# Joining softmax half rows with one-operand VectorE forms, and finishing the attention output on GpSimd

## The chip, the cores and the metric

The kernel runs on one core of a Trainium2 chip. The metric is device time in microseconds (us) from start to end of one execution. The engines named below are TensorE (PE in the profile, with its weight loads on a row of their own, PEld), VectorE (DVE), ScalarE (ACT), GpSimd (POOL) and the queue engine SyncE (SP), which here issues every DMA of the kernel. Each engine takes its instructions strictly in the order in which they stand; a semaphore wait of one instruction holds everything behind it on that engine.

## The reference, cut to what matters

Two independent results are put side by side. The left half is attention with 32 heads of 32 columns that share one key and one value head; the right half is a two-dimensional real Fourier mixing, written as matrix products.

```python
q = (x @ wq) split into 32 heads          # x: 2048 x 1024
k = x @ wk ; v = x @ wv                   # 2048 x 32 each
p = softmax(q k^T * 32**-0.5)             # per head, 2048 x 2048
a = concat_heads(p v) @ wo
y = Cr @ (xb @ Wr^T) - Ci @ (xb @ Wi^T)   # 2048 x 1024, Cr and Ci 2048 x 2048
out = concatenate([a, y], axis=-1)
```

## The kernel before, in words

All products outside the score and value products are made of three terms: an operand is cast to a rounded high part, the rest is its low part, and high·high, low·high and high·low are added in PSUM. In the profile's names `rh`, `rl` are the high and low part of a right operand, `mh`, `ml` of a left one.

The attention is cut into 32 units, one for each of four blocks of 512 queries (b) and eight groups of four heads (g). A unit passes through two loops of 32 steps each.

- The score loop, `score_step(s)`: a step makes the scores of 128 queries of one head against half of the 2048 keys (two matmuls into `pss`). VectorE takes the negative maximum of that half row into `nm` (a reduce of 128x1024 from PSUM). One step later ScalarE exponentiates the half row in place with that maximum as bias and leaves the sum of the half row in `ls`. So for each row there are two maxima and two sums.
- The join. When a unit's 32 score steps are through, its half rows are joined. The step number behind that is `e`: at e=1 `lse_1` finds the joint minimum of the negative maxima (`mm`) and the two differences (`md`); at e=2 `lse_1b` exponentiates the differences on ScalarE; at e=3 `lse_2` multiplies with the half sums, adds them (`l`), splits the joint maximum into a rounded and a low part and takes the reciprocal of the sum, all three into one tile `m`; at e=6 `lse_3` turns this tile with a TensorE transposition into a PSUM bank `psb` and VectorE copies it to `mt`; at e=8 `lse_4` sends two parts of `mt` by DMA into two rows of the query tile `qst` (so that the next product subtracts the maximum by itself) and the third part to memory.
- The value loop, `expo(n)` and `pv`: scores are made again, transposed (two matmuls into `pst`), exponentiated by ScalarE into `p`, and every eighth step the products with `v` go to `psb` and are added up in `ov` by VectorE. `expo` of unit u begins at e=12 of that unit, and its first matmul reads the two rows of `qst`. Score steps of the next unit and value steps of this one are recorded alternately, in one loop over n. After a unit's last `pv`, the next three steps take one entry each from the list `ends`: `ov` times 1/sum (`rb`, which the function `inverse` loads), the cast to the high part `oh`, and the low part `ol`. The low part's entry also records the stores of both parts on SP.

Between these steps the function `take` records the fill: about five matmuls per step of the other products (projections, the Fourier mixing, the output product), in groups of 24 or 12 matmuls to one PSUM bank. There are two such banks; the transposition and `pv` use them too. A group's result is taken out by VectorE. `aside()` runs before the transposition and before `pv`: close to a group's end it first takes the group's remaining matmuls, close to its begin the first six.

The fill's operands are prepared by two lines of due times (`RL`, `ML`, with leads counted in fill matmuls): SP loads a source into a staging tile, GpSimd adds or subtracts a second source where there is one (`r<-r,r`, `m<-m,m`), casts (`rh`, `mh`) and makes the low part (`rl`, `ml`). Left sources are loaded 52 matmuls ahead and prepared 36 to 21 ahead, right sources loaded and combined 40 ahead and finished 14 to 8 ahead. The staging tiles are few (`NR0, NM0 = 3, 3`), so a load on SP waits until GpSimd has made the low part of an earlier operand; all later DMAs stand behind that load. Stores stand nine fill matmuls behind the instruction that makes their data (`BEHIND = 9`). All engines but the DMA hardware keep program order.

Of the kernel before, what the change touches and what calls it, by code (L numbers as in the profile page):

```python
# [8 lines left out]
F32 = mybir.dt.float32  # L9
F32R = mybir.dt.float32r  # L10
AF = mybir.ActivationFunctionType
ALU = mybir.AluOpType
AX = mybir.AxisListType
# [3 lines left out]
P = 128  # L17
# [7 lines left out]
NC = 16  # L25
# [62 lines left out]
def tile_kernel(ctx: ExitStack, tc, xT, wq, wkv, wo, xbT, wT, cT, out):  # L88
    nc = tc.nc
    te = Ordered(tc, nc.tensor)  # L90
    act = Ordered(tc, nc.scalar)
    dve = Ordered(tc, nc.vector)
    gp = Ordered(tc, nc.gpsimd)
# [3 lines left out]
    def pool(stack, name, bufs, **kw):  # L97
        kw.setdefault("reuse_waits", "tile")
        return stack.enter_context(tc.tile_pool(name=name, bufs=bufs, **kw))
# [14 lines left out]
    ident = keep.tile([P, P], F32, name="ident")  # L114
# [17 lines left out]
    op = pool(ctx, "op", 2, side="right")  # L132
    hp = pool(ctx, "hp", 1, side="right")

    def move(q, to, of):
        q.dma_start(to.bitcast(F32), of.bitcast(F32))
# [181 lines left out]
    def store(to, of, key=None):  # L318
        def go():
            move(sp, to, of)  # L320
            if key:
                ready.add(key)
        soon(go)
# [4 lines left out]
    def bank(name, open_=False):  # L328

        b = 1 - cur["bank"] if cur["bank"] is not None else int(used[1] < used[0])  # L330
        cur["at"] += 1
        used[b] = cur["at"]
        if open_:
            cur["bank"] = b
        return ps_b[b].tile([P, W], F32, name=name)
# [42 lines left out]
    def aside():  # L378

        if cur["group"] >= len(groups):  # L380
            return
        g = groups[cur["group"]]
        j = pos["fill"] - g.at
        if 0 < j < 6:
            take(6 - j)
        elif j > g.n - 6:
            take(g.n - j)
# [193 lines left out]
    sm = pool(ctx, "sm", 2)  # L581
    onp = pool(ctx, "onp", 1)

    units = [(b, g) for b in range(NQ) for g in range(NG)]
# [3 lines left out]
    qst, nm, ls, lse, pt, ov, rb, pend = ({} for _ in range(8))  # L588
    ends = []

    def open_unit(u):
        b, g = units[u]
        assert ("q", b, g) in ready
        q = qsp.tile([P, 4, W], F32R, name="qst")
        gp.memset(q[96:P].bitcast(F32), 0.0)
        for r, src in enumerate((qh_d, ql_d, qh_d)):
            move(sp, q[r * DH:(r + 1) * DH], src[b][g].rearrange("(h d) c -> d h c", d=DH))
        qst[u] = q
        nm[u] = sm.tile([P, 2, NC], F32, name="nm")
        ls[u] = sm.tile([P, 2, NC], F32, name="ls")  # L600

    def scores(s):
        u, r = divmod(s, SU)
        i, j = divmod(r, 2)
        h, t = divmod(i, 4)
        ps = ps_s.tile([P, 2 * W], F32, name="pss")
        for a in range(2):
            k0 = (2 * j + a) * W
            te.matmul(ps[:, a * W:(a + 1) * W], qst[u][:, h, t * P:(t + 1) * P], kst[:, k0:k0 + W], start=True, stop=True)
        dve.tensor_reduce(nm[u][:, j, i:i + 1], ps, axis=AX.X, op=ALU.max, negate=True)  # L610
        pend[s] = ps

    def row_sums(s):
        if s not in pend:
            return
        ps = pend.pop(s)
        u, r = divmod(s, SU)
        i, j = divmod(r, 2)
        act.activation(ps, ps, AF.Exp, bias=nm[u][:, j, i:i + 1], accum_out=ls[u][:, j, i:i + 1])

    def lse_1(u):
        m = sm.tile([P, NC], F32, name="mm")
        d = sm.tile([P, 2, NC], F32, name="md")
        dve.tensor_tensor(m, nm[u][:, 0], nm[u][:, 1], op=ALU.min)
        for j in range(2):
            dve.tensor_sub(d[:, j], m, nm[u][:, j])
        lse[u] = m, d

    def lse_1b(u):
        act.activation(lse[u][1], lse[u][1], AF.Exp)  # L630

    def lse_2(u):
        m, d = lse[u]
        l = sm.tile([P, NC], F32, name="l")
        m2 = sm.tile([P, 3, NC], F32, name="m2")
        dve.tensor_mul(d, d, ls[u])
        dve.tensor_add(l, d[:, 0], d[:, 1])
        dve.tensor_copy(m2[:, 0].bitcast(F32R), m)
        dve.tensor_sub(m2[:, 1], m, m2[:, 0])
        dve.reciprocal(m2[:, 2], l)  # L640
        lse[u] = m2

    def lse_3(u):
        m2 = lse.pop(u)
        aside()
        pm = bank("psb")
        te.transpose(pm[:3 * NC, :P], m2.rearrange("p a b -> p (a b)"), ident)
        mt = sm.tile([3 * NC, P], F32, name="mt")
        dve.tensor_copy(mt, pm[:3 * NC, :P])
        cur["at"] += 1  # L650
        lse[u] = mt

    def lse_4(u):
        mt = lse.pop(u)
        for a in range(2):
            move(sp, qst[u][96 + a:97 + a].rearrange("o h (t c) -> o (h t) c", c=P), mt[a * NC:(a + 1) * NC])
        sp.dma_start(r_d[u], mt[2 * NC:])
# [16 lines left out]
    def pv(u, k):  # L674

        aside()
        ps = bank("psb")
        for c in range(4 * k, 4 * k + 4):
            for h in range(4):
                te.matmul(ps[h * DH:(h + 1) * DH], v[:, c], pt[u, c, h // 2][:, h % 2], start=c == 4 * k, stop=c == 4 * k + 3)  # L680
        if k == 0:
            ov[u] = onp.tile([P, W], F32, name="ov")
            dve.tensor_copy(ov[u], ps)
        else:
            dve.tensor_add(ov[u], ov[u], ps)
        cur["at"] += 1
        if k == NC // 4 - 1:
            b, g = units[u]
            hi_ = onp.tile([P, W], F32R, name="oh")
            lo_ = onp.tile([P, W], F32R, name="ol")  # L690
            lse["out"] = hi_, lo_

            def low():
                dve.tensor_sub(lo_, ov[u], hi_.bitcast(F32))
                if u + 1 < len(units):
                    store(oh_d[b][g], hi_)
                    store(ol_d[b][g], lo_, ("o", b, g))

            ends.append(lambda: dve.tensor_mul(ov[u], ov[u], rb[u]))
            ends.append(lambda: dve.tensor_copy(hi_, ov[u]))  # L700
            ends.append(low)

    def score_step(s):

        if s < total:
            u, r = divmod(s, SU)
            if r == SU - 6 and u + 1 < len(units):
                open_unit(u + 1)
            scores(s)
        row_sums(s - 1)  # L710
        u, e = divmod(s - SU, SU)
        if 0 <= u < len(units):
            if e == 1:
                lse_1(u)
            elif e == 2:
                lse_1b(u)
            elif e == 3:
                lse_2(u)
            elif e == 6:
                lse_3(u)  # L720
            elif e == 8:
                lse_4(u)


    room = [(lambda t=t, k=k: t[:, k]) for t in [pp.tile([P, 2, W], F32, name="p") for _ in range(9)] for k in range(2)]
    room += [(lambda t=t: t) for t in [hp.tile([P, W], F32, name=f"h{k}") for k in range(8)]]
# [5 lines left out]
    pump()  # L732
    take(START)
    open_unit(0)
    take(66)
    for s in range(SU + LEAD):
        score_step(s)
        take(7)
# [14 lines left out]
    for n in range(total):  # L753
        u, r = divmod(n, SU)
        if n == total - 12:
            w1 = wo_set(1)
            add([o_group(NQ - 1, t, e, ws) for e, ws in ((0, w0), (1, w1)) for t in range(4)])
        score_step(n + SU + LEAD)
        if ends:
            ends.pop(0)()  # L760
        expo(n)
        if r == 16:
            inverse(u)
        if r % 8 == 0 and n:
            pv(*divmod(n // 8 - 1, 4))
        level(n)


    last = groups[len(groups) - 8:]
    take(last[0].at - pos["fill"] - 12)  # L770
    pv(len(units) - 1, 3)
    while ends:
        ends.pop(0)()
# [65 lines left out]
```

## Time and profile before

| | us |
|---|---|
| three runs before | 2829.01, 2833.28, 2835.64; median 2833.28 |
| profiled execution, whole | 2835.39 |
| its span from first to last instruction | 2833.5 |
| PE busy in the span | 2780.5 (98%) |
| VectorE busy | 1733.6 (61%) |
| ScalarE busy | 2187.6 (77%) |
| GpSimd busy | 1481.7 (52%) |

The span is first to last instruction of the profiled execution, 1.9 us less than its own time. Every operation goes through one recording helper, so all have the line L66, and groups are told apart by tile names instead. A unit takes some 82 us. Units are counted from 0; unit 21 is the sixth head group of the third query block.

### The profile page before, as it was taken

The numbers are of one execution on the slowest core, as the hardware profiler recorded it, in microseconds if no ns is written. First come the engines' busy times: TensorE is split into PE (matmuls) and PEld (weight loads), VectorE is DVE, ScalarE is ACT, GpSimd is POOL, SyncE is SP. The second block draws the span as 40 slices with busy tenths as digits, with TensorE's granted clock in tenths as the row PEclk, the third lists the DMA queues.
The fourth block names the chain that finished last, engine by engine and source line by source line (L and its number), as shares of the span: only waits on it lengthen the run. The fifth ranks groups of instructions, "written<-read, shape, count | busy, mean of one in ns | idle before, by whom it ended". The sixth has DMA issues, their size and how long they took to land.

```text
span 2833.5 us, 40225 instructions
## 1 busy us (share of the span) xinstructions
PE 2780.5 (98%) x13904; PEld 1931.6 (68%) x13904; DVE 1733.6 (61%) x1925; ACT 2187.6 (77%) x3151; POOL 1481.7 (52%) x1433
## 2 busy tenths in 40 slices
PE   7999999999999999999999999999999999999999
PEld 5776666767666676767676766666666666767656
DVE  5766666666676666656665665666666566656511
ACT  4578888888888788888787877788878888888740
POOL 2321134565534447767685565787888765630010
PEclk9999999999999999999999999999999999999999
DMA  8865435775576455544463454564554543554445
GB/s 294 294 196 160 157 102 170 229 234 191 191 233 220 155 180 157 162 153 141 154 189 94 124 171 120 161 207 143 181 183 147 180 132 107 149 153 138 127 142 171
DMA packets 315724, 480.85 MB, mean 170 GB/s; under 512 B 33408, under 2 KB 98432, under 8 KB 315520
## 3 DMA queue, kind: packets, MB, share of 16 engines
q1 hardware_dynamic: 315520, 478.28, 53.5%
q8 instruction: 110, 1.80, 0.3%
q14 instruction: 94, 0.77, 0.1%
HBM read 364.12 MB, written 112.98 MB: 168 GB/s over the span
## 4 chain that ended last, share of the span: by engine, by line
PE 90%; DVE 3%; DMA 3%; ACT 1%; issue 1%; SPq 1%; POOL 0%; ACTq 0%; DVEq 0%; POOLq 0%
PE psb L66 57%; PE pss L66 17%; PE pst L66 16%; DVE nm L66 1%; SPq L66 1%; DMA s<-y 1%; DMA ql<-ql 1%; ACT p L66 1%; DVE md L66 1%; ACT pss L66 0%; DMA p<-in_xT_dram 0%; DVE mm L66 0%; DVE y L66 0%; DMA r<-s 0%; DMA r<-in_xT_dram 0%
## 5 line engine op out<-in xcount | busy, mean ns | idle before, releaser
L66 DVE TENSOR_REDUCE nm<-pss 128x1 f32<-128x1024 f32 x1024 | 1250.9, 1223 | 551.8 <-PE pss L66 550.8
L66 ACT ACTIVATE p<-pst 128x1024 f32<-128x1024 f32 x1024 | 1051.7, 1027 | 446.1 <-PE pst L66 442.9
L66 ACT ACTIVATE pss<-pss,nm 128x1024 f32<-128x1024 f32 x1024 | 1111.4, 1085 | 107.2 <-DVE nm L66 103.1
L66 PE MATMUL psb<-rh,mh 128*128 128x512 f32 (+1 forms) x1852 | 731.2, 395 | 18.2 <-ACT rh L66 8.2
L66 PE MATMUL psb<-rh,ml 128*128 128x512 f32 (+1 forms) x1852 | 730.4, 394 | 2.3 <-POOL ml L66 2.3
L66 PE MATMUL psb<-rl,mh 128*128 128x512 f32 (+1 forms) x1852 | 728.7, 393 | 0.3 <-DVE rl L66 0.3
L66 PE MATMUL pst<-qst,kst 128*128 128x512 f32 x2048 | 655.9, 401 | 14.0 <-ACT p L66 11.5
L66 PE MATMUL pss<-kst,qst 128*128 128x512 f32 x2048 | 656.2, 401 | 5.7 <-ACT pss L66 5.0
L66 PEld LDWEIGHTS pss<-kst,qst 128*128 128x128 f32 x2048 | 374.6, 188 | 190.1 <-issue 98.3
L66 PE MATMUL psb<-p,v 128*32 128x512 f32 x4096 | 467.9, 597 | 4.4 <-DVE h L66 3.0
L66 PEld LDWEIGHTS pst<-qst,kst 128*128 128x128 f32 x2048 | 373.7, 188 | 133.8 <-ACT p L66 45.1
L66 POOL CAST rh<-r 128x512 fp32r<-128x512 f32 x214 | 133.7, 625 | 550.4 <-PE psb L66 191.2
L66 PEld LDWEIGHTS psb<-rh,mh 128*128 128x128 f32 (+1 forms) x1852 | 346.9, 187 | 106.8 <-ACT rh L66 9.1
L66 POOL TENSOR_TENSOR ml<-m,mh 128x512 fp32r<-128x512 f32 x292 | 379.6, 1300 | 52.6 <-ACT mh L66 43.6
L66 PEld LDWEIGHTS psb<-rh,ml 128*128 128x128 f32 (+1 forms) x1852 | 346.8, 187 | 87.9 <-POOL ml L66 4.8
L66 PEld LDWEIGHTS psb<-rl,mh 128*128 128x128 f32 (+1 forms) x1852 | 347.0, 187 | 84.3 <-DVE rl L66 1.4
L66 POOL TENSOR_TENSOR r<-r,r 128x512 f32<-128x512 f32 x112 | 144.8, 1293 | 360.2 <-DMA r<-in_wT_dram 174.2
L66 PEld LDWEIGHTS psb<-p,v 128*32 128x32 f32 x4096 | 120.3, 110 | 282.5 <-issue 266.1
L66 POOL CAST mh<-m 128x512 fp32r<-128x512 f32 x291 | 182.8, 628 | 195.3 <-PE psb L66 175.2
L66 POOL TENSOR_TENSOR rl<-r,rh 128x512 fp32r<-128x512 f32 x214 | 276.3, 1292 | 5.8
L66 POOL TENSOR_TENSOR m<-m,m 128x512 f32<-128x512 f32 x192 | 248.4, 1294 | 46.2 <-DMA m<-in_xbT_dram 36.3
L66 DVE TENSOR_TENSOR ov<-ov,psb 128x512 f32<-128x512 f32 x96 | 66.0, 687 | 285.1 <-PE psb L66 285.1
(68 smaller groups left out, 955.3 us busy)
## 6 DMA issues: line engine op xcount, KB each, us to landing
m<-in_cT_dram SPq DMA_DIRECT2D x384, 256.0 KB, 3.8
r<-s SPq DMA_DIRECT2D x192, 256.0 KB, 4.4
y<-y SPq DMA_DIRECT2D x96, 256.0 KB, 4.4
r<-in_wT_dram SPq DMA_DIRECT2D x80, 256.0 KB, 3.7
m<-in_xbT_dram SPq DMA_DIRECT2D x80, 256.0 KB, 4.5
y<-u SPq DMA_DIRECT2D x80, 256.0 KB, 2.9
qst<-qh SPq DMA_DIRECT2D x64, 256.0 KB, 5.8
s<-y SPq DMA_DIRECT2D x64, 256.0 KB, 3.2
```

What stands on the lines that cost most here:

```text
L66: return lambda *a, **k: self.tc.keep_in_program_order(f(*a, **k))
```

## The change

The join is rewritten so that no VectorE instruction in it has two operands in SBUF. `nm` now has six rows of 16 columns: the two negative maxima, the joint maximum with its sign, and the three rows that are transposed. A view `over` puts the rows of a pair last, and a reduce over two elements does the work of a minimum, a difference or a sum. The product of the differences' exponentials with the half sums goes to GpSimd (`lse_1c`, at e=3). The VectorE part behind it moves from e=3 to e=6, the transposition from e=6 to e=7, and the DMAs of `lse_4` from e=8 to e=9. The three operations that finish a unit's output go to GpSimd for all units but the last.

```diff
-        nm[u] = sm.tile([P, 2, NC], F32, name="nm")
+        nm[u] = sm.tile([P, 6, NC], F32, name="nm")
...
+    def over(rows):
+        return rows.rearrange("p a c -> p c a")
+
     def lse_1(u):
-        m = sm.tile([P, NC], F32, name="mm")
+        z = nm[u]
         d = sm.tile([P, 2, NC], F32, name="md")
-        dve.tensor_tensor(m, nm[u][:, 0], nm[u][:, 1], op=ALU.min)
+        dve.tensor_reduce(z[:, 2], over(z[:, :2]), axis=AX.X, op=ALU.min, negate=True)
         for j in range(2):
-            dve.tensor_sub(d[:, j], m, nm[u][:, j])
-        lse[u] = m, d
+            dve.tensor_reduce(d[:, j], over(z[:, j::2 - j][:, :2]), axis=AX.X, op=ALU.add, negate=True)
+        lse[u] = d
...
+    def lse_1c(u):
+        gp.tensor_mul(lse[u], lse[u], ls[u])
+
     def lse_2(u):
-        m, d = lse[u]
+        z, d = nm[u], lse[u]
         l = sm.tile([P, NC], F32, name="l")
-        m2 = sm.tile([P, 3, NC], F32, name="m2")
-        dve.tensor_mul(d, d, ls[u])
-        dve.tensor_add(l, d[:, 0], d[:, 1])
-        dve.tensor_copy(m2[:, 0].bitcast(F32R), m)
-        dve.tensor_sub(m2[:, 1], m, m2[:, 0])
-        dve.reciprocal(m2[:, 2], l)
-        lse[u] = m2
+        dve.tensor_reduce(z[:, 3].bitcast(F32R), over(z[:, :2]), axis=AX.X, op=ALU.min)
+        dve.tensor_reduce(z[:, 4], over(z[:, 2:4]), axis=AX.X, op=ALU.add, negate=True)
+        dve.tensor_reduce(l, over(d), axis=AX.X, op=ALU.add)
+        dve.reciprocal(z[:, 5], l)
...
+            last = u + 1 == len(units)
+            e = dve if last else gp
+
             def low():
-                dve.tensor_sub(lo_, ov[u], hi_.bitcast(F32))
-                if u + 1 < len(units):
+                e.tensor_sub(lo_, ov[u], hi_.bitcast(F32))
+                if not last:
                     store(oh_d[b][g], hi_)
                     store(ol_d[b][g], lo_, ("o", b, g))
...
-            ends.append(lambda: dve.tensor_mul(ov[u], ov[u], rb[u]))
-            ends.append(lambda: dve.tensor_copy(hi_, ov[u]))
+            ends.append(lambda: e.tensor_mul(ov[u], ov[u], rb[u]))
+            ends.append(lambda: e.tensor_copy(hi_, ov[u]))
...
+    LSE = {1: (lse_1,), 2: (lse_1b,), 3: (lse_1c,), 6: (lse_2,), 7: (lse_3,), 9: (lse_4,)}
```

Three places in the order of instructions follow. The first is VectorE at the join of unit 21. Before (`nm<-pss` are the maxima of half rows, `psb` the bank that is taken out into `ov` or, for the transposition, into `mt`):

```order
L66 TENSOR_TENSOR mm<-nm 128x16
L66 TENSOR_TENSOR md<-mm,nm 128x16 x2
L66 TENSOR_TENSOR h_16637<-h_16637,psb 128x512
L66 TENSOR_REDUCE nm<-pss 128x1 x2
L66 TENSOR_TENSOR md<-md,ls 128x32
L66 TENSOR_TENSOR l<-md 128x16
L66 CAST m_17685<-mm 128x16
L66 TENSOR_TENSOR m_17685<-mm,m_17685 128x16
L66 RECIPROCAL m_17685<-l 128x16
```

and after:

```order
L66 TENSOR_REDUCE nm<-nm 128x16
L66 TENSOR_REDUCE md<-nm 128x16 x2
L66 TENSOR_TENSOR h_16597<-h_16597,psb 128x512
L66 TENSOR_REDUCE nm<-pss 128x1 x3
L66 TENSOR_TENSOR ov<-ov,psb 128x512
L66 TENSOR_REDUCE nm<-pss 128x1 x2
L66 TENSOR_REDUCE nm<-nm 128x16 x2
L66 TENSOR_REDUCE l<-md 128x16
L66 RECIPROCAL nm<-l 128x16
L66 TENSOR_REDUCE nm<-pss 128x1
L66 TENSOR_TENSOR h_16734<-h_16734,psb 128x512
L66 COPY mt<-psb 48x128
```

Five small instructions behind the second maximum have become four behind the fifth, and one maximum and one take-out stand between them and the copy of the transposition.

The second place is SP around the DMAs that carry the joined maximum of unit 21 into the query tile (`qst<-mt`). `m<-in_cT_dram` and `r<-s` are the loads of left and right sources, `y` partial results of the Fourier mixing. Before:

```order
L66 DMA m_17778<-in_cT_dram 128x512
L66 DMA m_17780<-in_cT_dram 128x512
L66 DMA y_17803<-y_0_7_280 128x512
L66 DMA y_17805<-y_1_7_288 128x512
L66 DMA qst<-mt 1x16x128 x2
L66 DMA r_150<-mt 16x128
L66 DMA r_17834<-s_8_358 128x512
```

and after:

```order
L66 DMA y_17750<-y_0_7_280 128x512
L66 DMA y_17752<-y_1_7_288 128x512
L66 DMA r_17787<-s_8_358 128x512
L66 DMA r_17789<-s_8_374 128x512
L66 DMA m_17792<-in_cT_dram 128x512
L66 DMA m_17794<-in_cT_dram 128x512
L66 DMA y_0_6_279<-y_17613 128x512
L66 DMA out_dram<-y_17615 128x512
L66 DMA qst<-mt 1x16x128 x2
L66 DMA r_150<-mt 16x128
```

The three small DMAs now stand behind two right sources, two left sources and two stores that followed them before.

The third is GpSimd after the change, where unit 20's output is finished (`ov`, `oh`, `ol`); the other rows stand there before as well, in the same order and without these three:

```order
L66 TENSOR_TENSOR ml<-m_17730,mh 128x512
L66 TENSOR_TENSOR ov<-ov,rb 128x512
L66 TENSOR_TENSOR r_17918<-r_17918,r_17920 128x512
L66 CAST mh<-m_17792 128x512
L66 CAST rh<-r_17787 128x512
L66 CAST oh<-ov 128x512
L66 TENSOR_TENSOR m_17842<-m_17842,m_17844 128x512
L66 TENSOR_TENSOR ml<-m_17792,mh 128x512
L66 TENSOR_TENSOR rl<-r_17787,rh 128x512
L66 TENSOR_TENSOR ol<-ov,oh 128x512
```

Between each two of the three stand operations that prepare the fill.

More of the change, by code (lines that the diff above doesn't have):

```diff
@@ L619, in row_sums @@
         act.activation(ps, ps, AF.Exp, bias=nm[u][:, j, i:i + 1], accum_out=ls[u][:, j, i:i + 1])
+    def over(rows):
+        return rows.rearrange("p a c -> p c a")
     def lse_1(u):
-        m = sm.tile([P, NC], F32, name="mm")
+        z = nm[u]
         d = sm.tile([P, 2, NC], F32, name="md")
-        dve.tensor_tensor(m, nm[u][:, 0], nm[u][:, 1], op=ALU.min)
+        dve.tensor_reduce(z[:, 2], over(z[:, :2]), axis=AX.X, op=ALU.min, negate=True)
         for j in range(2):
-            dve.tensor_sub(d[:, j], m, nm[u][:, j])
-        lse[u] = m, d
+            dve.tensor_reduce(d[:, j], over(z[:, j::2 - j][:, :2]), axis=AX.X, op=ALU.add, negate=True)
+        lse[u] = d
     def lse_1b(u):
-        act.activation(lse[u][1], lse[u][1], AF.Exp)
+        act.activation(lse[u], lse[u], AF.Exp)
+    def lse_1c(u):
+        gp.tensor_mul(lse[u], lse[u], ls[u])
     def lse_2(u):
-        m, d = lse[u]
+        z, d = nm[u], lse[u]
         l = sm.tile([P, NC], F32, name="l")
-        m2 = sm.tile([P, 3, NC], F32, name="m2")
-        dve.tensor_mul(d, d, ls[u])
-        dve.tensor_add(l, d[:, 0], d[:, 1])
-        dve.tensor_copy(m2[:, 0].bitcast(F32R), m)
-        dve.tensor_sub(m2[:, 1], m, m2[:, 0])
-        dve.reciprocal(m2[:, 2], l)
-        lse[u] = m2
+        dve.tensor_reduce(z[:, 3].bitcast(F32R), over(z[:, :2]), axis=AX.X, op=ALU.min)
+        dve.tensor_reduce(z[:, 4], over(z[:, 2:4]), axis=AX.X, op=ALU.add, negate=True)
+        dve.tensor_reduce(l, over(d), axis=AX.X, op=ALU.add)
+        dve.reciprocal(z[:, 5], l)
     def lse_3(u):
-        m2 = lse.pop(u)
         aside()
         pm = bank("psb")
-        te.transpose(pm[:3 * NC, :P], m2.rearrange("p a b -> p (a b)"), ident)
+        te.transpose(pm[:3 * NC, :P], nm[u][:, 3:].rearrange("p a b -> p (a b)"), ident)
         mt = sm.tile([3 * NC, P], F32, name="mt")
@@ L712, in score_step @@
         if 0 <= u < len(units):
[L713 to L722, printed above, removed]
+            for f in LSE.get(e, ()):
+                f(u)
+    LSE = {1: (lse_1,), 2: (lse_1b,), 3: (lse_1c,), 6: (lse_2,), 7: (lse_3,), 9: (lse_4,)}
     room = [(lambda t=t, k=k: t[:, k]) for t in [pp.tile([P, 2, W], F32, name="p") for _ in range(9)] for k in range(2)]
```

## The prediction

> **What bounds the kernel now.** I read the page first, its busy times and its chain of waits.
>
> ```profile
> span 2833.5 us, 40225 instructions
> PE 2780.5 (98%) x13904; PEld 1931.6 (68%) x13904; DVE 1733.6 (61%) x1925; ACT 2187.6 (77%) x3151; POOL 1481.7 (52%) x1433
> PE 90%; DVE 3%; DMA 3%; ACT 1%; issue 1%; SPq 1%; POOL 0%; ACTq 0%; DVEq 0%; POOLq 0%
> ```
>
> TensorE is the bound, and neither VectorE's 61% nor GpSimd's 52% can lengthen or shorten anything except through a TensorE stall. So the change is priced in TensorE stalls alone. Those of the two loops are counted in the windows and in TensorE's waits, both for 80 to 2700 us.
>
> ```profile
> 80.00:2700.00 2620.00, 2591.73 (x13055) 1805.33 (x13055) 1671.46 (x1833) 2119.64 (x3063) 1441.60 (x1385) 1.00 0.53 166
> PE pst L66 <- ACT p L66: 11.5, 14, 4.3
> PE psb L66 <- DVE h L66: 4.7, 4, 2.3
> PE psb L66 <- DVE y L66: 2.5, 2, 1.3
> PE psb L66 <- POOL ml L66: 2.5, 2, 1.3
> ```
>
> The first row has the stretch, then TensorE's busy time: 2620.0 - 2591.7 = 28.3 us idle in 2620. The others have the sum of a wait, how often, and the longest. No faster VectorE can bring more than those 28 us and the time in which the clock was down after a stall.
>
> Next, what makes them. These are the groups by form of the operations that the change touches (busy us in all, mean ns of one, idle before).
>
> ```profile
> L66 DVE TENSOR_TENSOR mm<-nm 128x16 f32<-128x16 f32 x32 | 18.7, 586 | 0.0
> L66 DVE TENSOR_TENSOR md<-mm,nm 128x16 f32<-128x16 f32 x64 | 26.6, 456 | 1.1
> L66 DVE TENSOR_TENSOR md<-md,ls 128x32 f32<-128x32 f32 x32 | 11.3, 354 | 2.8 <-ACT md L66 2.8
> L66 DVE TENSOR_TENSOR l<-md 128x16 f32<-128x16 f32 x32 | 15.7, 492 | 1.1
> L66 DVE CAST m<-mm 128x16 fp32r<-128x16 f32 x32 | 12.3, 384 | 0.0
> L66 DVE TENSOR_TENSOR m<-mm,m 128x16 f32<-128x16 f32 x32 | 14.9, 464 | 1.1
> L66 DVE RECIPROCAL m<-l 128x16 f32<-128x16 f32 x32 | 7.8, 244 | 0.0
> L66 DVE TENSOR_TENSOR ov<-ov,rb 128x512 f32<-128x512 f32 x32 | 26.7, 836 | 0.1
> L66 POOL TENSOR_TENSOR ml<-m,mh 128x512 fp32r<-128x512 f32 x292 | 379.6, 1300 | 52.6 <-ACT mh L66 43.6 <-PE psb L66 4.4
> L66 POOL CAST mh<-m 128x512 fp32r<-128x512 f32 x291 | 182.8, 628 | 195.3 <-PE psb L66 175.2 <-DMA m<-in_xbT_dram 13.2 <-DMA m<-in_wq_dram 5.4
> ```
>
> A subtraction over 16 columns takes 456 ns on average, twice a reciprocal over the same 16. The worst case shows why (start, duration, engine).
>
> ```profile
> 1686.93 1.28 POOL L66 TENSOR_TENSOR ml<-m,mh 128x512 fp32r<-128x512 f32 x1
> 1687.25 5.78 DVE L66 TENSOR_TENSOR mm<-nm 128x16 f32<-128x16 f32 x1
> 1691.74 1.26 POOL L66 TENSOR_TENSOR rl<-r,rh 128x512 fp32r<-128x512 f32 x1
> 1694.56 1.22 PE L66 MATMUL pst<-qst,kst 128*128 128x512 f32 x2 [4.31 <-ACT p L66]
> ```
>
> The 16-column minimum began under one GpSimd operation and ended at 1693.03 with the last of an unbroken row of them. Maxima stood behind it, ScalarE behind those, and TensorE lost 4.31 us. The granted clock (the column after the busy times) went down after that stall, and after one of 2.3 us at 1782.
>
> ```profile
> 1694.50:1698.00 3.50, 3.44 (x8) 2.77 (x9) 2.39 (x7) 2.85 (x5) 1.24 (x2) 0.50 0.31 110
> 1698.00:1702.00 4.00, 4.00 (x28) 1.40 (x31) 1.23 (x1) 2.49 (x5) 1.84 (x2) 0.74 0.23 70
> 1785.00:1790.00 5.00, 5.00 (x32) 1.16 (x28) 0.94 (x1) 1.21 (x2) 2.02 (x3) 0.66 0.68 255
> ```
>
> **The change part by part: the joins.** Seven VectorE instructions per unit stay seven. Without GpSimd beside them such forms take what the reciprocal takes or less, so lse_1 and lse_2 should cost 0.5 and 0.8 us wherever they fall. The stalls that go: of the row `PE pst <- ACT p` all but the small ones, 10.5 of 11.5 us. Of the rows `DVE h` and `DVE y` the three stalls ahead of value products behind a stretched lse_2: the longest of each, 2.3 and 1.3, and one of 0.8 at 2363, 4.4 us. The waits for 2355 to 2370 us have the last one alone:
>
>
> ```profile
> PE psb L66 <- DVE h L66: 0.8, 1, 0.8
> ```
>
> And the clock: 0.50 of 3.5 us, 0.26 of 4 us and 0.34 of 5 us, 1.75 + 1.04 + 1.7 = 4.5 us. Sum 19.4 us. If one-operand forms waited for GpSimd like the old ones, 0; all idle time and the clock, 28 + 5, is the other end. I stay with 19.4, since each term is a stall whose cause stands beside it.
>
> A rule of the Trainium skill bears on that. Its page SBUF — State Buffer, section Who interferes with whom, says that a VectorE instruction with two SBUF inputs contends with a GpSimd instruction that reads SBUF, that on this chip a tensor_reduce never does, and that the loser waits for the whole of the other's instruction. By it the new joins are free of waits, as summed. By its last part no join would wait longer than one GpSimd instruction, 1.3 us, and the 4.31 us stall and its clock, 4.31 + 2.79 = 7.1 us, would not be there to be won; the sum below would then be +6.2 us. The 5.78 us row differs from that, and the row decides.
>
> **The output on GpSimd.** 31 units times (1.30 + 0.63 + 1.30) = 100 us more on GpSimd, plus a 32-column product, which I bound between VectorE's reciprocal over half as many, 0.244, and GpSimd's 1.30 over sixteen times as many; being nearer to the first in size, I take 0.25, 8 us. VectorE gets 0.84 us and its two neighbours back; few TensorE stalls follow those steps, 0 to 3 us, I take 1. Where GpSimd has idle time the added 3.5 us per 82 us unit cost nothing: its work leads its use. The cover is gone where GpSimd is behind.
>
> ```profile
> 1804.00:1886.00 82.00, 81.99 (x416) 56.89 (x415) 51.54 (x56) 68.52 (x100) 70.22 (x67) 1.00 0.65 205
> SPq L66 <- POOL ml L66: 98.3, 24, 8.0
> ```
>
> GpSimd is busy 70.2 of 82 us there, and SP's waits for 1800 to 1970 us (second row) have 98 of 170 us for GpSimd's low parts. What it is late with, SP's whole queue is late with.
>
> **The DMAs that move a step.** They decide the forecast. Unit 21 and unit 23 before:
>
> ```profile
> 1883.81 1.15 SPq L66 DMA_DIRECT2D qst<-mt  x2
> 1887.95 0.70 PE L66 MATMUL pst<-qst,kst 128*128 128x512 f32 x2 [1.51 <-DMA qst<-mt]
> 1889.82 0.43 SPq L66 DMA_DIRECT2D out_dram<-y  x1
> 2047.29 1.15 SPq L66 DMA_DIRECT2D qst<-mt  x2
> 2052.33 0.43 SPq L66 DMA_DIRECT2D out_dram<-y  x1
> 2052.28 0.63 PE L66 MATMUL pst<-qst,kst 128*128 128x512 f32 x2
>   DMA to landing us min/median/max: 1.6/2.1/4.4
> ```
>
> At unit 21 TensorE already waits 1.51 us for this DMA. By the new order it stands behind the store that was issued at 1889.82, so it goes out at 1890.25 instead of 1883.81: 6.4 us more stall, in full. At unit 23 it goes out at 2052.76 instead of 2047.29 and lands, with 4.2 us of the row's 4.4, at 2057.0; the product that needs it started at 2052.28: 4.7 us. Elsewhere SP is not behind and the margin of a median landing stays three steps wide. To this come GpSimd's two added outputs ahead of unit 21, 6.5 us, of which its idle time takes most: I put 1.5 us. Two stalls of that size bring the clock down, 1.75 us each, 3.5 us. A TensorE that is later waits less for `ml` behind it: -1.3 us. Sum 14.8 us. Bounds: 0, if SP is not late in this execution, and 30, if each of some nine heavily loaded units passes on its 3.5 us.
>
> **The transposition one step behind the join.** It had three steps, now one. The rows of unit 21 show what a step leaves.
>
> ```profile
> 1872.36 0.63 PE L66 MATMUL pss<-kst,qst 128*128 128x512 f32 x2
> 1873.03 1.23 DVE L66 TENSOR_REDUCE nm<-pss 128x1 f32<-128x1024 f32 x1 [1.09 <-PE pss L66]
> 1874.78 0.63 PE L66 MATMUL pss<-kst,qst 128*128 128x512 f32 x2
> ```
>
> A score pair ends its maximum at 1874.26; with 0.8 us for lse_2 the tile is ready at 1875.05. The next pair starts at 1874.78, and 0.46 us later, at 1875.24, TensorE wants to transpose, with a weight load of the tile 0.23 us ahead. So nothing is left over. I take 0.15 us a unit, 4.7 us; ends are 0 (a transposition often stands behind fill matmuls that `aside` took) and a 0.7 us take-out ahead of the maximum in each, 21 us. The bank conflict behind a transposition stays: it stands right behind a group's last matmul in six units before and seven after.
>
> **Sum.** -19.4 - 1 + 14.8 + 4.7 = -0.9 us on an execution of 2835.39 us (span 2833.5 and 1.9 around it). That execution lies 2.1 us above the median of 2833.28, so I put the median after at 2832.
>
> **The rivals.** (a) The stretch from 1800 to 2060 us charges nothing: GpSimd, no longer held by VectorE's 512-column operations, is less late than before, and only the transposition costs. Then -20.4 + 4.7 = -15.7: 2818. For it speaks that a lateness which comes once in the run can fail to come; against it the 98 us of SP waits. (b) Slower: GpSimd's lateness is passed on in every heavily loaded unit. Nine units at 3.5 us are 31 us instead of 14.8, the sum +15.3: 2849. It makes the kernel slower by over 0.2% once 21.4 us are passed on (20.4 - 4.7 + 5.7), six units. For it speaks that SP's loads wait for the very operations that come later; against it GpSimd's 12 us idle in the row above. (c) The change doesn't do what it says: reduces over pairs in SBUF wait for GpSimd like the 16-column cast, which has one operand too and averages 384 ns. Then the joins bring nothing and the costs stay: 2833.3 - 1 + 14.8 + 4.7 = 2852. The reciprocal, one operand and 244 ns with nothing lost, speaks against it. By the rule of the Trainium skill's page SBUF — State Buffer weighed above, it would not happen.
>
> **How the numbers follow.** No change is what lies within 0.2%, 5.7 us, about what three runs with a spread of 6.6 us can tell. My own sum has 0.42: within its 8 us either side 0.24 are same, 0.09 faster, 0.09 slower. (a) has 0.29, all faster. (b) has 0.23 and (c) 0.06, all slower. So faster 0.38, same 0.24, slower 0.38. The range goes from the whole gain without any cost, 2833.3 - 20.4 = 2813, less a microsecond, to (b), 2849; the forecast's own range is 2824 to 2840.
>
> **What would show it.** Right on the joins: every `md`, `l` and `nm<-nm` near 0.2 us, `PE pst <- ACT p` under 2 us, no 0.50 clock at unit 19. Right on the DMAs: `PE pst <- DMA qst<-mt` at units 21 and 23, 10 us or more in all. Right on the transposition: a new wait of the load of `nm` under the identity for VectorE, some 5 us. Wrong if VectorE's reduces stand for over 1 us, if the `qst<-mt` wait is under 3 us, or if TensorE waits for `ml` and `rl` in many units.

## The result and the profile after

The changed kernel takes 2815.62 us (median of four runs, 2814.74 to 2816.89) beside 2831.79 us for the kernel before in the same series (2829.01 to 2835.64): ratio 0.9942, 95% interval 0.9925 to 0.996. It is faster by 16 us. The profiled execution takes 2816.89 us. First its page, then the window of the two loops:

```profile
span 2815.0 us, 40144 instructions
PE 2776.0 (99%) x13904; PEld 1935.7 (69%) x13904; DVE 1612.9 (57%) x1800; ACT 2182.6 (78%) x3151; POOL 1569.4 (56%) x1558
```

```profile
80.00:2700.00 2620.00, 2604.73 (x13145) 1819.74 (x13144) 1553.87 (x1713) 2123.90 (x3071) 1529.06 (x1510) 1.00 0.54 167
```

TensorE is idle for 15.3 us of these 2620, where it was 28.3. Its waits in the same stretch (sum, times, longest) say what went and what came:

```profile
PE pst L66 <- DMA qst<-mt: 4.7, 1, 4.7
PE psb L66 <- DVE nm L66: 2.5, 3, 1.7
PE psb L66 <- DVE y L66: 1.8, 2, 1.0
PE psb L66 <- DVE h L66: 1.5, 2, 1.0
PE psb L66 <- POOL ml L66: 0.5, 1, 0.5
PE pst L66 <- ACT p L66: 0.3, 1, 0.3
```

The wait of the transposed scores for ScalarE, 11.5 us before, is gone (0.3). Those for the take-outs (`h`, `y`) fell from 7.2 to 3.3 us. Larger is the stall for the DMA of the joined maximum, 4.7 us where it was 1.5; new are 2.5 us for the joined tile itself (`nm`). The joins by form (busy us, mean ns of one):

```profile
L66 DVE TENSOR_REDUCE nm<-nm 128x16 f32<-128x32 f32 x64 | 11.7, 183 | 1.1
L66 DVE TENSOR_REDUCE md<-nm 128x16 f32<-128x32 f32 x64 | 9.0, 183 | 1.1
L66 DVE TENSOR_REDUCE l<-md 128x16 f32<-128x32 f32 x32 | 5.7, 178 | 2.7 <-POOL md L66 2.7
L66 POOL TENSOR_TENSOR md<-md,ls 128x32 f32<-128x32 f32 x32 | 8.1, 253 | 160.8 <-ACT md L66 160.0 <-PE psb L66 0.8
```

A reduce over 16 pairs takes 0.18 us everywhere, where the subtractions took 0.46 on average and the minima 0.59. GpSimd's new product takes 0.253 us. The DMA's stall and the longest of the three for the tile both fall in unit 21. First the tile (start, duration, engine; the number in brackets is the idle time before):

```profile
1856.75 0.25 POOL L66 TENSOR_TENSOR md<-md,ls 128x32 f32<-128x32 f32 x1
1857.03 0.19 DVE L66 TENSOR_REDUCE l<-md 128x16 f32<-128x32 f32 x1 [2.12 <-POOL md L66]
1857.56 0.29 PE L66 MATMUL psb<-ident,nm 128*48 128x128 f32 x1 [1.66 <-DVE nm L66]
```

GpSimd is late with the product, VectorE stands 2.12 us for it, and TensorE 1.66 us for VectorE. Then the DMA:

```profile
1863.20 0.90 SPq L66 DMA_DIRECT2D y<-y  x2
...
1871.16 0.43 SPq L66 DMA_DIRECT2D out_dram<-y  x1
1871.69 1.71 SPq L66 DMA_DIRECT2D qst<-mt  x2
1876.03 1.19 PE L66 MATMUL pst<-qst,kst 128*128 128x512 f32 x2 [4.72 <-DMA qst<-mt]
```

It goes out behind the store, as the order said, 8.5 us behind the loads `y<-y`, and lands late. At unit 23 the DMAs go out 4.5 us ahead of the product that needs them, and the profile shows no wait:

```profile
2035.70 1.14 SPq L66 DMA_DIRECT2D qst<-mt  x2
2040.19 0.73 PE L66 MATMUL pst<-qst,kst 128*128 128x512 f32 x2
```

The granted clock goes down around both stalls of unit 21:

```profile
1860.00:1875.00 15.00, 11.31 (x43) 8.71 (x41) 6.74 (x6) 8.86 (x14) 13.14 (x13) 0.84 0.66 213
1875.00:1890.00 15.00, 13.97 (x68) 8.54 (x69) 4.30 (x4) 7.86 (x11) 14.17 (x15) 0.83 0.42 140
```

That is 15 x 0.16 + 15 x 0.17 = 4.9 us, about what the clock took at units 19 and 20 before: the prediction's windows give 4.5, windows that begin before those stalls (1690 to 1710 and 1780 to 1790 us) give 5.2.

### The profile page after: what moved, and what is told of

It reads as the page before. It is cut to its first block, busy times and chain, and to the rows that moved or that the text cites. A ratio compares the mean times of both kernels' runs of the same rounds, so it can differ in the third digit from the quotient of the medians.

```text
span 2815.0 us, 40144 instructions
## 1 busy us (share of the span) xinstructions
PE 2776.0 (99%) x13904; PEld 1935.7 (69%) x13904; DVE 1612.9 (57%) x1800; ACT 2182.6 (78%) x3151; POOL 1569.4 (56%) x1558
## 4 chain that ended last, share of the span: by engine, by line
PE 93%; DMA 2%; POOL 1%; issue 1%; DVE 1%; SPq 1%; ACT 1%; POOLq 0%; DVEq 0%; ACTq 0%
PE psb L66 59%; PE pss L66 18%; PE pst L66 17%; DMA r<-s 1%; DMA ql<-ql 1%; SPq L66 1%; POOL ml L66 0%; DMA r<-in_xT_dram 0%; DVE nm L66 0%; POOL mh L66 0%; POOL m L66 0%; DMA wq<-mh 0%; POOL rl L66 0%; POOL rh L66 0%; POOL y L66 0%
```

## The experiments

Times are medians of at least four runs, ratios are to the kernel before on the same chip. The question is which part of the change brings the 16 us, and which part gives something back.

**The joins without the output.** The output's three operations go back to VectorE.

```diff
-            e = dve if last else gp
+            e = dve
```

> The changed kernel with the output's three operations back on VectorE; joins, product on GpSimd and later steps stay. Theory (the gain is VectorE's waits for GpSimd in the joins): nearly the whole gain, 2811 to 2820 us, with TensorE's wait for ScalarE's p under 1 us; GpSimd 97 us less busy. Rival (the gain is VectorE freed of the output): 2828 us or more.

Measured: 2816.04 us, ratio 0.9949 (0.9933 to 0.9966), the time of the whole change. One execution of the four is longer, 2822.71 us (the others 2814.47 to 2816.7), and it is the profiled one. It shows one thing that the others need not have had. Its timeline at 1880 us (start, duration, engine):

```profile
1881.90 8.54 DVE L66 TENSOR_TENSOR ov<-ov,rb 128x512 f32<-128x512 f32 x1
1881.97 0.62 POOL L66 CAST mh<-m 128x512 fp32r<-128x512 f32 x1
...
1888.62 1.28 POOL L66 TENSOR_TENSOR ml<-m,mh 128x512 fp32r<-128x512 f32 x1
1891.67 1.09 ACT L66 ACTIVATE pss<-pss,nm 128x1024 f32<-128x1024 f32 x1 [7.34 <-DVE nm L66]
```

and TensorE's wait behind it:

```profile
PE pss L66 <- ACT pss L66: 6.4, 1, 6.4
```

A product of two SBUF operands that takes 0.68 us in most units (the median of the 32) stands 8.54 us here, from one GpSimd operation to the end of an unbroken row of eight. ScalarE misses its maximum for 7.3 us, TensorE stands 6.4. The wait for `qst<-mt` is 4.4 us in this trace, so it doesn't hang on where the output is finished.

**The output alone.** The kernel before, with only the output on GpSimd.

```diff
-            ends.append(lambda: dve.tensor_mul(ov[u], ov[u], rb[u]))
-            ends.append(lambda: dve.tensor_copy(hi_, ov[u]))
+            ends.append(lambda: e.tensor_mul(ov[u], ov[u], rb[u]))
+            ends.append(lambda: e.tensor_copy(hi_, ov[u]))
```

> The kernel before with the output's three operations on GpSimd and nothing else; joins in two-operand forms at their old steps. Theory: no gain, 2830 to 2842 us, joins waiting at least as long as before (77 us over their quiet durations, output included). Rival (output frees VectorE): 2815 to 2822 us.

Measured: 2828.58 us, ratio 0.9998 (0.9988 to 1.0007). The old joins still stall TensorE:

```profile
PE pst L66 <- ACT p L66: 8.5, 16, 2.0
PE psb L66 <- DVE h L66: 4.7, 4, 2.3
```

So the output on GpSimd brings nothing that the runs can tell, alone or on top of the joins. The gain comes with the rewritten joins.

**The later steps alone.** The kernel before with its old two-operand joins, at the steps that the change uses.

```diff
-            elif e == 3:
+            elif e == 6:
                 lse_2(u)
-            elif e == 6:
+            elif e == 7:
                 lse_3(u)
-            elif e == 8:
+            elif e == 9:
```

> The kernel before with lse_2, the transposition and the DMAs at steps 6, 7 and 9 and nothing else. Theory: the later steps bring nothing and cost TensorE a longer wait for the DMA into qst about 1870 to 1890 us, 2832 to 2845 us. Rival (the gain is luck of the new places between the fill groups): 2815 to 2825 us.

Measured: 2852.31 us, ratio 1.0082 (1.0067 to 1.0098), 22 us slower than the series' kernel before by the medians.

```profile
PE psb L66 <- DVE m L66: 16.2, 10, 3.5
PE pst L66 <- ACT p L66: 8.6, 14, 1.4
PE pst L66 <- DMA qst<-mt: 6.2, 1, 6.2
```

With one step between join and transposition, ten of the old joins stall TensorE (`m` is the old joined tile, 16.2 us). So the tight place costs little only because the new forms keep their time. From this kernel to the one with new joins (2816.04) are 36 us. The reverse, new forms at the old steps 3, 6 and 8, was not run.

**Is it the form?** Four more instructions per unit behind `lse_1`, whose result nobody uses, once as minima of two operands, once as reduces over pairs.

```diff
+    def lse_x(u):
+        x = sm.tile([P, NC], F32, name="x")
+        for _ in range(4):
+            dve.tensor_tensor(x, nm[u][:, 0], nm[u][:, 1], op=ALU.min)
-    LSE = {1: (lse_1,), ...
+    LSE = {1: (lse_1, lse_x), ...
```

> Adds, behind the three reduces of lse_1 in each unit, four minima with two operands over 16 columns whose result nobody uses. Theory (a two-operand operation is held by a GpSimd that runs without a gap, and what stands behind it on VectorE is late): such operations stand for 0.45 to 0.6 us on average and for 3 to 8 us in some unit, the wait of the transposed weights for exponentials is back, and the time is 2820 to 2840 us. Rival (what counted in the old joins was the number of instructions and their place): the time is that of the kernel with four added reduces, within 0.1%, and at most 2819 us.

The other kernel has this line in its place:

```diff
-            dve.tensor_tensor(x, nm[u][:, 0], nm[u][:, 1], op=ALU.min)
+            dve.tensor_reduce(x, over(nm[u][:, :2]), axis=AX.X, op=ALU.min)
```

> The same place and number as the kernel with four added minima, but as reduces over pairs with one operand. Theory: each takes 0.17 to 0.19 us everywhere, 0.7 us a unit, no TensorE wait is added, 2813 to 2818 us. Rival (a longer VectorE queue is what costs): as slow as with the two-operand forms.

Measured: 2848.96 us (ratio 1.0066, 1.0048 to 1.0083) with two operands, 2818.07 us (0.9957, 0.994 to 0.9974) with one. The same number of instructions in the same place differs by 31 us. The group of the added instructions with two operands, then a unit's four at 2282 us with what runs beside them and waits for them:

```profile
L66 DVE TENSOR_TENSOR x<-nm 128x16 f32<-128x16 f32 x128 | 51.0, 398 | 3.3
```

```profile
2282.66 4.07 DVE L66 TENSOR_TENSOR x<-nm 128x16 f32<-128x16 f32 x4
2282.68 1.29 POOL L66 TENSOR_TENSOR y<-y,h 128x512 f32<-128x512 f32 x1
...
2283.94 1.30 POOL L66 TENSOR_TENSOR m<-m,m 128x512 f32<-128x512 f32 x1
...
2285.18 1.30 POOL L66 TENSOR_TENSOR ml<-m,mh 128x512 fp32r<-128x512 f32 x1
2286.65 2.35 DVE L66 TENSOR_REDUCE nm<-pss 128x1 f32<-128x1024 f32 x2
```

and the group with one operand:

```profile
L66 DVE TENSOR_REDUCE x<-nm 128x16 f32<-128x32 f32 x128 | 23.7, 185 | 3.3
```

51.0 - 23.7 = 27 us more of VectorE's time go with 31 us of the kernel's. The traces carry most of these: TensorE is idle 18.4 us longer in the loops (35.1 beside 16.6), and the granted clock costs 5.1 us more (8.5 beside 3.4, summed over windows of 10 us). The idle time comes by another way than I expected: not as the wait of `pst` for `p`, but as that of the scores for ScalarE,

```profile
PE pss L66 <- ACT pss L66: 17.1, 15, 2.4
```

since the maxima behind the four instructions are late. The bound of 2840 us that I gave was too low, by 9 us. The rival (number and place count) falls. The two kernels differ in the operation (`tensor_tensor`, `tensor_reduce`) as well as in the number of operands; they don't separate the two.

**The product back on VectorE.**

```diff
-        gp.tensor_mul(lse[u], lse[u], ls[u])
+        dve.tensor_mul(lse[u], lse[u], ls[u])
```

> The product of exponentials with half sums back on VectorE, at the same step. It is then the one two-operand operation left in the join. Theory: 0.35 us on average with a stretched one in a heavy unit, but VectorE no longer waits for a late GpSimd at unit 21 (the 1.8 us stall of the transposition there goes), 2812 to 2822 us. Rival (moving the product is a large part of the gain): 2825 us or more.

Measured: 2813.98 us, ratio 0.9941 (0.9926 to 0.9956), not to be told from the whole change. The product (min/median/max ns) is held in some units, at most for one GpSimd operation:

```profile
L66 DVE TENSOR_TENSOR md<-md,ls x32: 179/243/1332, 145.0 to 2660.5; 128x32 f32<-128x32 f32 x32
```

TensorE's stall for the joined tile at unit 21 is gone as expected, but the stall for the DMA that follows it has grown by 2.9 us:

```profile
PE pst L66 <- DMA qst<-mt: 7.6, 1, 7.6
```

The landing stands in SP's queue; a TensorE that comes earlier only waits longer for it.

**The transposition a step later**, at 8 instead of 7.

```diff
-    LSE = {..., 6: (lse_2,), 7: (lse_3,), 9: (lse_4,)}
+    LSE = {..., 6: (lse_2,), 8: (lse_3,), 9: (lse_4,)}
```

> The transposition a step later, at 8, two steps behind the join, the DMAs stay at 9. By the prediction's term for the transposition, 0.15 us in each unit, this would bring 4.7 us: 2811 us. By the trace after, in which TensorE loses some 1 to 2 us to the copy of the joined tile, 1 to 2 us: 2814 us; if the copy to the DMA is then too close, the DMA of unit 21 is later still and it is 2816 to 2819 us.

Measured: 2820.43 us, ratio 0.9962 (0.9947 to 0.9977), slower than the change by the medians. The last of the three cases came, for the same reason as above:

```profile
PE pst L66 <- DMA qst<-mt: 10.7, 2, 8.1
2042.64 0.71 PE L66 MATMUL pst<-qst,kst 128*128 128x512 f32 x2 [2.52 <-DMA qst<-mt]
```

The wait for `nm` is gone, that for the DMA is 6.0 us longer: 8.1 us at unit 21 and, in the second row, 2.5 us at unit 23. So the price of the transposition's place can't be read from this kernel.

**The DMAs a step earlier**, at 8 instead of 9.

```diff
-    LSE = {..., 6: (lse_2,), 7: (lse_3,), 9: (lse_4,)}
+    LSE = {..., 6: (lse_2,), 7: (lse_3,), 8: (lse_4,)}
```

> The changed kernel with lse_4's DMAs one step earlier, at step 8. Theory (the DMA's wait is SP's lateness behind GpSimd): the 4.7 us wait for qst<-mt falls to under 2 us and the time by 2 to 6 us, to 2810 to 2814 us. Rival (GpSimd's lateness at 1860 us comes out at another wait, for nm or ml): the wait moves, the time stays within 1.5 us of 2815.6.

Measured: 2810.8 us, ratio 0.9931 (0.9916 to 0.9946), 4.8 us under the change by the medians. SP at unit 21:

```profile
1860.74 0.90 SPq L66 DMA_DIRECT2D y<-y  x2
1861.74 1.15 SPq L66 DMA_DIRECT2D qst<-mt  x2
...
1868.70 0.43 SPq L66 DMA_DIRECT2D out_dram<-y  x1
```

The DMAs go out 1.0 us behind the loads `y<-y`, where it was 8.5 us, and the wait for them isn't in the list any more. The intervals of the two ratios overlap; that the DMAs' wait is what went rests on the trace.

**The DMAs on another queue.** Step 9 stays, ScalarE issues them.

```diff
-            move(sp, qst[u][96 + a:97 + a]...
+            move(act, qst[u][96 + a:97 + a]...
```

> The two DMAs of the joined maximum are issued on ScalarE's queue instead of SP's, at the same step 9. Theory (unit 21's stall is SP's lateness behind GpSimd, handed on): the wait for these DMAs is gone without moving any step, 2809 to 2813 us. Rival (the step is too late in itself, whatever the queue): the wait of 4.7 us stays and the time is 2814 to 2818 us. If the 64 issues on ScalarE cost it time ahead of the exponentials, the wait of the transposed weights for exponentials grows and it is 2815 us or more.

Measured: 2857.58 us, ratio 1.0096 (1.008 to 1.0112): 42 us slower than the change. The wait for the DMAs did go, and a far larger one came. The waits, then ScalarE and TensorE at unit 21:

```profile
PE pst L66 <- ACT p L66: 32.6, 11, 7.4
```

```profile
1881.11 5.85 ACTq L66 DMA_DIRECT2D qst<-mt  x2
...
1887.01 1.02 ACT L66 ACTIVATE p<-pst 128x1024 f32<-128x1024 f32 x1 [7.90 <-DMA m<-in_cT_dram]
...
1888.09 1.22 PE L66 MATMUL pst<-qst,kst 128*128 128x512 f32 x2 [7.44 <-ACT p L66]
```

Each issue takes 0.52 us, but the second stands until 1886.4, and the exponentials stand behind it. The profile puts ScalarE's wait down to a load that SP had issued (`m<-in_cT_dram`). Why an issue on ScalarE is held by a load of SP's wasn't tried; whether the chip holds it or a semaphore of the program isn't shown. Up to 1300 us the second issue stands at most 0.6 us; from 1375 us on it stands 1.3 to 4.9 us in nine units, 32 us in all, which is TensorE's wait. Much of the rest of the 42 us is the clock: over windows of 10 us it costs 22 us in the loops, where it was 5.

**The join's second half at step 5, the DMAs at 8**, so that the transposition at 7 has two steps.

```diff
-    LSE = {..., 6: (lse_2,), 7: (lse_3,), 9: (lse_4,)}
+    LSE = {..., 5: (lse_2,), 7: (lse_3,), 8: (lse_4,)}
```

> The join's second half at step 5, the transposition at 7, the DMAs at 8: against the kernel with the DMAs at step 8 (2810.8 us) only the transposition's distance to the join grows from one step to two. By the prediction's term for that distance 4.7 us less, 2806 us; by the trace, where the copy of the joined tile holds TensorE 1.8 us in all, 2808 to 2811 us. Rival: the sum over the halves now waits one step less for the product on GpSimd, which is late at unit 21, so VectorE stands there longer and TensorE with it, 2811 to 2815 us.

Measured: 2806.18 us, ratio 0.9915 (0.9901 to 0.9928), the lowest median of all. Against the kernel with only the DMAs at 8 that is 4.6 us less, the prediction's whole term, but the intervals of the two ratios overlap, and the trace doesn't carry so much:

```profile
80.00:2700.00 2620.00, 2609.29 (x13193) 1821.07 (x13192) 1554.97 (x1712) 2126.41 (x3073) 1529.27 (x1509) 1.00 0.53 168
PE psb L66 <- DVE nm L66: 1.5, 1, 1.5
```

10.7 us idle in the loops, where the kernel with the DMAs at 8 has 12.6. Two of the three stalls for `nm` are gone, the one at unit 21 is left: it is GpSimd's product, not the distance. The same steps with the product on VectorE as well:

```diff
-    LSE = {..., 6: (lse_2,), 7: (lse_3,), 9: (lse_4,)}
+    LSE = {..., 5: (lse_2,), 7: (lse_3,), 8: (lse_4,)}
-        gp.tensor_mul(lse[u], lse[u], ls[u])
+        dve.tensor_mul(lse[u], lse[u], ls[u])
```

> The same steps with the product on VectorE, so that nothing of the join waits for GpSimd. Theory: the stall of the transposition at unit 21 is gone in any case, 2806 to 2810 us. Rival (the one two-operand form is stretched at unit 21 or later and costs as much as the wait saved): 2810 to 2814 us.

Measured: 2807.35 us, ratio 0.992 (0.9907 to 0.9934). The wait for `nm` is gone and the time is the same; the wait for `ml` has grown from 1.1 to 1.8 us, and one of 0.7 us for the DMA has come up.

**The output of five units on VectorE**, with the DMAs at step 8.

```diff
-            e = dve if last else gp
+            e = dve if last or 18 <= u <= 22 else gp
```

> DMAs at step 8, and the output of the five units 18 to 22 back on VectorE. Theory (the added 3.2 us a unit make GpSimd later in the stretch from 1480 to 1890 us, which shows in the stalls of 1.5 us at 1853 and 1.4 us at 1927): these go, 2806 to 2810 us. Rival (a two-operand operation over 512 columns between GpSimd operations without a gap is held for several of them, as with the output of unit 20 when all of it is on VectorE, 8.5 us): a stall of 3 to 7 us by 1890 us and 2812 to 2818 us.

Measured: 2809.72 us, ratio 0.9928 (0.9915 to 0.9942), beside 2810.8 without. No difference that can be told. The stall for `nm` at unit 21 shrinks but the one for `ml` stays:

```profile
PE psb L66 <- POOL ml L66: 1.2, 1, 1.2
PE psb L66 <- DVE nm L66: 1.2, 2, 0.8
```

So the 3.2 us a unit that the output adds to GpSimd explain little of the lateness in this stretch.

## Why the prediction was right in its range and off in its likeliest case

The time lies in the predicted range of 2812 to 2849 us, but outside the forecast's own 2824 to 2840: it is 16 us off the likeliest value, and 2 us off rival (a), the case in which the stretch from 1800 to 2060 us charges nothing. That it comes so near to (a) is luck, since the stretch did charge 6.1 us, the transposition cost less than (a) had, and 3 us of the gain have no known place. The step that failed is the sum for the DMAs that move a step, 14.8 us; the transposition was over-priced too.

- **The joins, -19.4: right.** The wait for `p` fell by 11.2 us (10.5 forecast), those for `h` and `y` by 3.9 (4.4), and the clock losses at units 19 and 20 (4.5) are gone. That the form is the cause is shown twice: 31 us between added instructions of one form and the other, 36 us between the old joins at the later steps and the new ones there. Rival (c), reduces that wait too, is out: 0.17 to 0.19 us in every unit. The rule of the Trainium skill (SBUF — State Buffer, Who interferes with whom) that a reduce doesn't contend holds in these runs. Its other part, that the loser waits for the whole of the other's instruction, taken as one instruction, fits the product on VectorE (1.33 us at most) and fails at the 8.54 us row, as it did at the 5.78 us row before.
- **The output, -1: too small to tell.** Neither run that isolates it shows a gain or a loss, and their intervals are wider than 1 us.
- **The DMAs, +14.8: mis-sized.** The place and the mechanism were right for unit 21, behind the store and late, but TensorE lost 4.7 us instead of 1.5, so 3.2 more, where I had put 6.4 + 1.5. At unit 23 I had put 4.7 us and nothing came: the wait for these DMAs occurs once, where the prediction's sign for this step was 10 us or more at two units. The clock's 4.9 us (3.5 forecast) came at unit 21 alone, part of it behind the stall for the tile. `ml` fell by 2.0 (1.3). Together 3.2 + 4.9 - 2.0 = 6.1 us. What I did wrong was to add the lateness of SP as it stood in one trace to a step moved within it, at two units one after the other. The same shift in two kernels says what the step is worth: with the old joins 6.2 us instead of 1.5, with the new ones 4.7 instead of none with the DMAs at step 8. At unit 23 the DMAs went out 4.5 us ahead of the product (2035.70 and 2040.19 above), where I had put them 0.5 us behind it. Why SP is that much less late there stays open. That the stall at unit 21 lets GpSimd catch up isn't enough as a reason: with the transposition at step 8 that stall was 8.1 us, and unit 23 waited 2.5 us all the same.
- **The transposition, +4.7: over-priced, and of another make.** The wait for `nm` is 2.5 us in three units (some 5 us were forecast), not 0.15 us in each. Two of the three go with one more step of distance, the third, 1.7 us, is GpSimd's product being late, which I had costed only as 8 us of GpSimd's idle time, without asking who waits for it: VectorE does, and the transposition behind it.
- **The bank conflicts: unchanged, as forecast.** These are waits of the next group behind a transposition for the bank that is being taken out. The waits for `h` and `y` that are left are of that kind, 0.5 to 1.0 us each.
- **The clock:** the forecast "no 0.50 at unit 19" came true, and the loss reappeared at unit 21 in about equal size.

The sum with the measured terms, in the loops: -11.2 - 3.9 - 2.0 (`ml`) + 3.2 + 2.5 - 1.6 for the other small waits (5.0 before, 3.4 after) is -13.0, the difference of the idle times; the clock's -4.5 and +4.9 nearly cancel. Of the other 3 us of the medians' 16, or 5.5 of the 18.5 between the two profiled executions, I can't say where they lie.

## What to carry to other kernels

Beside a GpSimd that works without a gap, a small VectorE operation should have a form that keeps its time, even if it has to be a reduce over a pair. One operand by itself isn't the test: the reduces and the reciprocal kept theirs, but the old join's 16-column cast, with one operand too, took 0.16 to 1.33 us. The share of VectorE's busy time doesn't show what such an instruction costs when a maximum or an exponential stands behind it. A stall that stands ahead of a late transfer can't be won by itself, since TensorE then waits longer for the transfer; first the latest event is moved (here the DMAs, 4.8 us by the medians), then what stands ahead of it. And a lateness read from one trace is priced once, not at each unit that follows.

## What the hardware showed that I had not expected

- A VectorE product with two SBUF operands was held 8.54 us across eight GpSimd operations in a row, while four small ones behind each other took 4.07 us, 1.0 us each, and none of the 128 took more than 1.35 us. Both occur; what decides between them stayed open.
- 64 DMA issues moved to ScalarE cost 42 us, though each took 0.52 us: the second of a pair stood up to 4.9 us, which the profile puts down to DMAs that SP had issued.
- The granted clock went down behind the stalls of unit 21 (0.84 and 0.83 over 15 us each), which were 1.7 and 1.0 us within 3 us, and 4.7 us. With the DMAs a step earlier, where the longest wait in the loops was 1.3 us, the loops show no such place:

```profile
1860.00:1875.00 15.00, 14.41 (x78) 9.21 (x77) 7.58 (x8) 10.70 (x16) 13.34 (x13) 1.00 0.56 180
PE psb L66 <- DVE nm L66: 1.8, 2, 1.3
```
